# Feature maps of a linear attention: the negative exponentials and the reciprocals moved to GpSimd as powers of -1

## The chip, the cores and the metric

The kernel runs on one core of one Trainium2 chip. The metric is the device time of one execution in microseconds. Three runs of the kernel before gave 747.75, 748.07 and 748.65 us; their median is 748.07 us.

## The reference

Two attention blocks read the same `x` (2048 rows of 512 features, 32 heads of 16) and a gate mixes their outputs. Block A is a linear attention with a feature map of two softmaxes; block B is plain softmax attention. Cut to what matters:

```python
def _A_ref(x, wqkv, w_phi, wo):
    q, k, v = split_heads(x @ wqkv)              # each [B, 32, 2048, 16]
    pq = jnp.einsum("bhsd,hdf->bhsf", q, w_phi)
    pk = jnp.einsum("bhsd,hdf->bhsf", k, w_phi)
    phi_q = jnp.concatenate([_softmax(pq), _softmax(-pq)], axis=-1)   # 32 features of a head
    phi_k = jnp.concatenate([_softmax(pk), _softmax(-pk)], axis=-1)
    kv  = jnp.einsum("bhsf,bhsd->bhfd", phi_k, v)
    z   = jnp.einsum("bhsf->bhf", phi_k)
    num = jnp.einsum("bhqf,bhfd->bhqd", phi_q, kv)
    den = jnp.einsum("bhqf,bhf->bhq", phi_q, z)[..., None] + 1e-6
    return merge_heads(num / den) @ wo

def _B_ref(x, wqkv, wo):
    q, k, v = split_heads(x @ wqkv)
    p = _softmax(jnp.einsum("bhqd,bhkd->bhqk", q, k) * 0.25)
    return merge_heads(jnp.einsum("bhqk,bhkd->bhqd", p, v)) @ wo

g = sigmoid((x * gate_w).sum(-1, keepdims=True))
return g * _A_ref(...) + (1 - g) * _B_ref(...)
```

## The kernel before

**Block B** is most of the work. It is cut into 32 sets (four blocks of 512 queries, four groups of eight heads, two halves of a group), and a set into 16 key tiles of 128 keys. For a key tile TensorE makes four scores of [128 keys, 512 queries] in PSUM (L1106), something turns them into exponentials, and TensorE multiplies them with the values into `psO` (L1143). A key tile is done in one of two ways:

- ScalarE: two exponentials of 128x1024 elements from PSUM into `E` tiles (L1116); then four matmuls with the values.
- VectorE: four operations of 128x512 elements from PSUM write the exponent's bits straight into an int16 tile `T` (L1121), two more of 128x2048 elements from SBUF to SBUF add shifts to it (L1129, tiles `TS`, called "sh" in the code), and three groups of four matmuls add up the three versions.

Up to six key tiles of a set (`DSET`) may go either way; a planner decides.

**Block A** runs beside it. The function `phi` makes a feature map of 128 rows: TensorE projects them (`fill`, L787, tile of 128x512 in PSUM), ScalarE makes exp(P) and exp(-P) in two operations (L979) into the two halves of a bf16 tile of 128x1024, GpSimd sums groups of 16 by halving in four additions (L985, L990, L991, L992), VectorE takes the reciprocals of the 64 sums (L994), and GpSimd multiplies the tile by them (L995). `phi` is called 16 times for the keys (tiles `phk`; their results go to the matmuls of L1018, in four batches) and then 16 times for the queries (tiles in the place of `WAT`; their results are transposed by a DMA and go to the matmuls of L1055).

**The order.** The whole program is recorded as operations with a cost and a priority, and `_Sched` orders it before it is built. `STYLES` holds one seed for each 4 us of the plan; a seed draws the tolerances by which TensorE's next operation is picked in that window (0 is the standard style). Each engine then runs its own queue in that fixed order, with semaphores between engines. The planner knows of a path that GpSimd shares with the shift operations of VectorE: it does not place an operation of GpSimd into the time of a shift, places one that it takes to be longer than `LONG` (0.8 us) close behind a shift (`NEAR`, `HOLD`), and makes the operation of GpSimd wait for the last shift planned ahead of it. A shift is not made to wait for GpSimd:

```python
            elif o.eng == "pool":
                if self.sh and self.sh[-1] not in o.deps and self.sh[-1].end > w - 20.0:
                    o.deps.append(self.sh[-1])
                self.port["pool"] = w + occ + PORT
            elif o.kind == "sh":
                self.sh.append(o)
                self.port["dve"] = w + occ + PORT
```

A general path for large inputs stands behind a flag at the end of the program; with the inputs here it isn't taken.

Of the kernel before, what the change touches and what calls it, by code (L numbers as in the profile page):

```python
# [7 lines left out]
F32 = mybir.dt.float32  # L8
I16 = mybir.dt.int16
I32 = mybir.dt.int32  # L10
ACTF = mybir.ActivationFunctionType
ALU = mybir.AluOpType
# [31 lines left out]
NE_, NPH = 12, 6  # L44
WINDOW = 4.0
STYLES = (
# [11 lines left out]
LEAD = {"act": 1.1, "dve": 1.0}  # L58
NE = "dve"
PORT, LONG, NEAR, HOLD = 0.05, 0.8, 0.3, 6.0  # L60
# [41 lines left out]
class _Sched:  # L102
# [5 lines left out]
    def add(self, eng, prio, occ, fn, deps=(), tiles=(), mode=None, name="", lat=None, dma=None, lane=None, nb=0.0,  # L108
            kind=None, run=None, alt=None):
        o = _Op()  # L110
        o.alt = alt
        o.eng, o.fn, o.occ, o.prio = eng, fn, occ, prio
        o.lat = {"pe": 0.17, "act": 0.12, "dve": 0.09, "pool": 0.1, "sp": 0.0}[eng] if lat is None else lat
        if dma is not None:
            o.lat = dma
        o.deps = [d for d in deps if d is not None]
        o.tiles = list(tiles)
        o.mode, o.name, o.dma, o.lane, o.est, o.kind, o.run = mode, name, dma, lane, nb, kind, run
        o.users, o.start, o.end, o.count, o.sem, o.vc = [], None, None, None, None, None
        o.seq = len(self.ops)  # L120
        for t in o.tiles:
            t.ops.append(o)
        self.ops.append(o)
        return o
# [502 lines left out]
def _build(ctx, nc, A_x, A_wqkv, A_w_phi, A_wo, B_wqkv, B_wo, gate_w, out):  # L627
    cnt = [0]

    def sb(shape, dt=BF16, name="sb"):  # L630
        cnt[0] += 1
        return ctx.enter_context(nc.sbuf_tensor(f"{name}_{cnt[0]}", shape, dt))
# [5 lines left out]
    add = sch.add  # L638
# [21 lines left out]
    omg = sb([128, NT], F32, name="omg")  # L660
    ct = sb([128, 112], F32, name="ct")
    flag = sb([128, 1], I32, name="flag")

    qst_r = ring(2, [128, NQ], name="qst")
    qz_r = ring(2, [128, 4, NQ], name="qz")
# [49 lines left out]
    def x_in(c, deps=()):  # L715
# [12 lines left out]
                  deps=[xin[1]], name=f"x{c}", dma=8.5) for c in (2, 3)]  # L728
# [5 lines left out]
    def pool(prio, occ, fn, deps=(), name="", tiles=(), alt=None, nb=0.0):  # L734
        return add("pool", prio, occ, fn, deps=deps, name=name, tiles=tiles, alt=alt, nb=nb)
# [8 lines left out]
    z3 = pool(-99.4, 0.2, lambda e: e.tensor_single_scalar(ta, ta, 16.0, ALU.is_lt), [z2])  # L744
    z4 = pool(-99.3, 0.2, lambda e: e.tensor_tensor(ta, ta, tb, ALU.mult), [z3])
    op_qm = pool(-99.2, 0.2, lambda e: e.tensor_tensor(qmask[:], ta[:, 0:4], ta[:, 4:8], ALU.add), [z4])
    op_ones = pool(-99.05, 0.3, lambda e: e.memset(ones[:], 1.0))
    op_qz0 = [pool(-60, 1.8, lambda e: e.memset(qz_r.aps[1 - q_t[0, 0].idx], 0.0))]
    vfl = vB[:].rearrange("p t h c -> p (t h) c")
# [5 lines left out]
                  name="wphi", lane=lambda: ("wphi", 0)) for j in range(8)]  # L755
# [48 lines left out]
    for c in range(2):  # L804
        got = []
        for t in range(KT):
# [3 lines left out]
            f = chain((-100, XT1)[c], calls, 0.11, [xin[c], op_id], [m, xs[c]], "xt")  # L810
# [91 lines left out]
    for w in range(2):  # L902
        for t in range(KT):
            tile = _Tile(M_r)
            prio = st_(WP0 + 0.12 * (4 * w + t))
# [7 lines left out]
            f = add("pe", prio, 0.3, fn, deps=[op_wat] + op_wbd, tiles=[tile], mode="full", name="wp", nb=prio - EARLY)  # L913
# [19 lines left out]
    for c in range(QC):  # L933
        m, f = sumsq(st_(CX0 + 0.3 * c), lambda hh, c=c: xT[:, 2 * hh:2 * hh + 2, NQ * c:NQ * (c + 1)], op_x[c], "x")
        cert.append(add("dve", st_(CX0 + 0.2 + 0.3 * c), 0.62, lambda e, m=m, c=c: e.tensor_reduce(ct[:, c:c + 1], m.ap, AX.X, ALU.max),
                        deps=[f], tiles=[m]))
    for i, (w, dp) in enumerate(((W_Bq, [op_wq[0], op_wq[1]]), (W_Bk, [op_wk[0], op_wk[1]]))):
        m, f = sumsq(st_(CW0 + 0.3 * i), lambda hh, w=w: w[:, 2 * hh:2 * hh + 2, :], dp, "w")
# [3 lines left out]
    for w in range(2):  # L942
        m, f = sumsq(st_(CP0 + 0.3 * w), lambda hh, w=w: Wp[:, w, 2 * hh:2 * hh + 2, :], ev_wp[w], "p")
# [27 lines left out]
    def phi(prio, w, st, ee, ee_deps):  # L971
        tile, ss, tr = _Tile(M_r), _Tile(ss_r), _Tile(tr_r)
        f = fill(prio, tile, 0, lambda t: xT[:, t, 128 * st:128 * (st + 1)], lambda t: Wp[:, w, t, :],
                 ev_wp[0] + ev_wp[1] + op_x[st // 4] + ee_deps, f"pf{w}{st}", [ee])
        if w == 1:
            use_wp1.append(f)
        P = lambda: tile.ap.rearrange("p (h f) -> p h f", f=DH)
        ev = lambda: ee.ap.rearrange("p (h f) -> p h f", f=32)
        ex = [add("act", prio, 0.48, lambda e, s=s: e.activation(ev()[:, :, 16 * s:16 * s + 16], P(), ACTF.Exp, scale=1.0 - 2.0 * s),  # L979
                  deps=[f] + ee_deps, tiles=[tile, ee]) for s in range(2)]  # L980
        eg = lambda: ee.ap.rearrange("p (g f) -> p g f", f=DH)
        v8 = lambda: tr.ap[:, 0:512].rearrange("p (g f) -> p g f", f=8)
        v4 = lambda: tr.ap[:, 0:256].rearrange("p (g f) -> p g f", f=4)
        v2 = lambda: tr.ap[:, 256:384].rearrange("p (g f) -> p g f", f=2)
        p1 = pool(prio + 2, 1.23, lambda e: e.tensor_tensor(v8(), eg()[:, :, 0:8], eg()[:, :, 8:16], ALU.add), ex + use_wat,  # L985
                  tiles=[ee, tr], name="ps1")
        tr2 = _Tile(tr2_r)
        u4 = lambda: tr2.ap[:, 0:256].rearrange("p (g f) -> p g f", f=4)
        u2 = lambda: tr2.ap[:, 256:384].rearrange("p (g f) -> p g f", f=2)
        p2 = pool(prio + 2, 0.92, lambda e: e.tensor_tensor(u4(), v8()[:, :, 0:4], v8()[:, :, 4:8], ALU.add), [p1], tiles=[tr, tr2])  # L990
        p3 = pool(prio + 2, 0.56, lambda e: e.tensor_tensor(u2(), u4()[:, :, 0:2], u4()[:, :, 2:4], ALU.add), [p2], tiles=[tr2])  # L991
        p4 = pool(prio + 2, 0.48, lambda e: e.tensor_tensor(ss.ap[:, 0, :], u2()[:, :, 0], u2()[:, :, 1], ALU.add), [p3],  # L992
                  tiles=[tr2, ss])
        o7 = add("dve", prio + 5, 0.46, lambda e: e.reciprocal(ss.ap[:, 1, :], ss.ap[:, 0, :]), deps=[p4], tiles=[ss])  # L994
        return pool(prio + 6, 1.95, lambda e: e.tensor_tensor(  # L995
            eg(), eg(), ss.ap[:, 1, :].unsqueeze(2).to_broadcast([128, 64, DH]), ALU.mult),
            [o7], tiles=[ee, ss], name="phi")
# [3 lines left out]
    for qd in range(4):  # L1001
        items = []
        for i in range(4):
            st = 4 * qd + i
            prio = st_(PK0 + PK1 * st)
            ph, va = _Tile(phk_r), _Tile(vA_r)
            op = phi(prio, 1, st, ph, [])
            tile = _Tile(M_r)
            f = fill(prio + 2, tile, 0, lambda t, st=st: xT[:, t, 128 * st:128 * (st + 1)], lambda t: W_Av[:, t, :],
                     op_x[st // 4] + [op_wav] + op_vAones, "vAf", [va])  # L1010
            use_wav.append(f)
            ev = add("dve", prio + 2, 0.62, lambda e, va=va, tile=tile: e.tensor_copy(
                va.ap[:, :, 0:64], tile.ap.rearrange("p (g c) -> p g c", c=64)), deps=[f] + op_vAones, tiles=[tile, va], name="vAev")
            items.append((ph, va, op, ev))
        for lo in (0, 4):
# [5 lines left out]
            f = chain(st_(PK0 + 0.5 + PK1 * (4 * qd + 3)), calls, 0.06, [x[2] for x in items] + [x[3] for x in items],  # L1021
                      [tkv] + [x[0] for x in items] + [x[1] for x in items], "kv", 0.0, 4 * PIECE)
# [5 lines left out]
            else:  # L1028
                kvo.append(add("dve", pr, 0.38, lambda e, dst=dst, src=src: e.tensor_tensor(dst, src(), dst, ALU.add),
                               deps=[f] + kvo, tiles=[tkv]))  # L1030
# [9 lines left out]
    for st in range(NT):  # L1040
        x = PQ0 + PQ1 * st if st < 4 else PQ2 + PQ3 * (st - 4)
        prio = st_(x)
        ph, ptt, rA, oA, nd = _Tile(eA_r), _Tile(phT_r), _Tile(rA_r), _Tile(oA_r), [_Tile(M_r), _Tile(M_r)]
        nd[0].mate, nd[1].mate = nd[1], nd[0]
        if st % 4 == 0:
# [4 lines left out]
                 deps=[op_ph] + use_wp1, tiles=[ph, ptt], name="phT", dma=2.6, lane=lambda ptt=ptt, st=st: (("phT", ptt.idx), st))  # L1050

        def nums(e, ptt=ptt, nd=nd):
# [8 lines left out]
            deps=[o3, op_ge], tiles=[rA] + nd, name="den")  # L1061
# [5 lines left out]
            deps=[o5] + use_wav, tiles=[nd[b], rA, oA], name="oA") for b in range(2)]  # L1067
# [11 lines left out]
    for s in range(N_SETS):  # L1079
# [12 lines left out]
        for eng, frac, kt in todo:  # L1092
# [4 lines left out]
            for cc in range(2):  # L1097
# [5 lines left out]
                def qk(e, rs=rs, c=c, kt=kt, g=g, qt=qt):  # L1103
                    ins = None
                    for h in range(2):
# [4 lines left out]
                        name=f"qk{s}.{kt}", kind="qk", run=eng, alt=alt)  # L1110
# [119 lines left out]
    for o in sch.order["pe"]:  # L1230
        if o.kind == "pv":
            s, key = o.run
# [71 lines left out]
```

## Time and profile before

| | |
|---|---|
| median of three runs | 748.07 us |
| the profiled execution | 749.46 us, its span 747.6 us |
| granted TensorE clock, mean | 0.992 |
| ScalarE, busy | 711.6 us (95%) |
| TensorE matmuls, busy | 695.1 us (93%) |
| VectorE, busy | 693.4 us (93%) |
| GpSimd, busy | 193.7 us (26%) |
| ScalarE's exponentials of block B (L1116) | 726 of 128x1024 |
| VectorE's shifts (L1129) | 298 of 128x2048 |
| ScalarE's exponentials of the feature maps (L979) | 64 of 128x512 |
| VectorE's reciprocals of their sums (L994) | 32 of 128x64 |

How the profile's lines are read: PE is TensorE, PEld its weight loads, DVE VectorE, ACT ScalarE, POOL GpSimd. A line of a group reads: source line, engine, operation, tile written<-tile read, partitions x elements, count | busy us, mean ns of one | idle time of the engine just before them, and what ended it. In a timeline the first number is the start in us from the span's start and the second the time in us; "xN" merges N of the same kind in a row. Operations of one engine overlap at their ends, so what one costs its queue is the distance from its start to the next one's start.

### The profile page before, as it was taken

How to read it: one execution, taken by the hardware profiler on the slowest of the kernel's cores; microseconds unless marked ns; L12 is line 12 of the kernel's file. 1: busy time of each engine (PE TensorE's matmuls, PEld its weight loads, DVE VectorE, ACT ScalarE, POOL GpSimd, SP SyncE). 2: the span in 40 equal slices, each digit the busy share in tenths (PEclk: the TensorE clock that was granted, in tenths of full speed). 3: DMA queues.
4: the chain of work that ended last, by engine and by line, in shares of the span. 5: the costliest groups of instructions: out<-in, count | busy, mean ns of one | idle time of the engine just before them, and what ended most of it. 6: DMA issues, size and time to landing. Idle time of an engine off the chain costs nothing.

```text
span 747.6 us, 15606 instructions
## 1 busy us (share of the span) xinstructions
PE 695.1 (93%) x6432; PEld 216.0 (29%) x6432; DVE 693.4 (93%) x1212; ACT 711.6 (95%) x803; POOL 193.7 (26%) x234
## 2 busy tenths in 40 slices
PE   7999999999999989988989999998989999988886
PEld 3333342332322222222222332222222322222222
DVE  3989899999999999999999999999999999999993
ACT  3999799999999999999999999999999999999993
POOL 4165241233344343322322012222212112200000
PEclk8999999999999999999999999999999999999999
DMA  8300000011000000001211221211111211111001
GB/s 210 73 16 9 8 16 15 15 41 33 15 15 15 8 14 10 15 16 30 48 31 30 50 50 36 44 33 33 22 36 40 47 36 37 32 27 8 16 8 32
DMA packets 72157, 23.77 MB, mean 32 GB/s; under 512 B 64016, under 2 KB 72080, under 8 KB 72080
## 3 DMA queue, kind: packets, MB, share of 16 engines
q1 hardware_dynamic: 70736, 22.19, 13.9%
q8 instruction: 52, 0.85, 0.5%
q10 hardware_dynamic: 1344, 0.52, 0.3%
q14 instruction: 25, 0.20, 0.1%
HBM read 4.21 MB, written 2.10 MB: 8 GB/s over the span
## 4 chain that ended last, share of the span: by engine, by line
ACT 65%; PE 26%; DVE 5%; DMA 2%; SPq 1%; issue 0%; DVEq 0%
ACT E L1116 62%; PE psR L1106 10%; PE psO L1143 6%; PE psR L787 4%; PE psR L1205 3%; DVE T L1121 2%; PE psR L849 2%; ACT WAT L979 2%; ACT phk L979 1%; DMA OTT<-OT 1%; DVE TS L1129 1%; SPq L706 1%; DMA T<-in_A_x_dram 1%; PE psR L927 1%; DVE ob L1170 1%
## 5 line engine op out<-in xcount | busy, mean ns | idle before, releaser
L1116 ACT ACTIVATE E<-psR 128x1024 bf16<-128x1024 f32 x726 | 679.8, 1120 | 17.2 <-PE psR L1106 15.8
L1121 DVE TENSOR_SCALAR T<-psR 128x512 int16<-128x512 f32 x596 | 380.8, 683 | 20.8 <-PE psR L1106 16.3
L1106 PE MATMUL psR<-qz,kT 64*128 64x512 bf16 x2048 | 347.5, 386 | 38.3 <-ACT E L1116 28.0
L1129 DVE TENSOR_SCALAR TS<-T 128x2048 int16<-128x2048 int16 x298 | 193.2, 684 | 3.1
L1106 PEld LDWEIGHTS psR<-qz,kT 64*128 64x128 bf16 x2048 | 87.0, 93 | 306.6 <-ACT E L1116 221.3
L1143 PE MATMUL psO<-E,vB 128*18 128x512 bf16 x1452 | 127.1, 382 | 0.0
L1143 PE MATMUL psO<-TS,vS 128*18 128x512 bf16 x1192 | 105.6, 382 | 0.6 <-DVE TS L1129 0.6
L1143 PE MATMUL psO<-T,vB 128*18 128x512 bf16 x596 | 58.7, 384 | 0.0
L985 POOL TENSOR_TENSOR WAT<-WAT 128x512 f32<-128x512 bf16 x16 | 18.5, 1156 | 148.0 <-DVE TS L1129 105.6
L990 POOL TENSOR_TENSOR tr<-WAT 128x256 f32<-128x256 f32 x32 | 23.4, 733 | 94.5 <-DVE TS L1129 94.5
L1143 PEld LDWEIGHTS psO<-E,vB 128*18 128x18 bf16 x1452 | 31.3, 88 | 51.3 <-issue 37.1
L995 POOL TENSOR_TENSOR phk<-phk,ss 128x1024 bf16<-128x1024 bf16 x16 | 30.9, 1930 | 51.5 <-DVE TS L1129 51.5
L995 POOL TENSOR_TENSOR WAT<-WAT,ss 128x1024 bf16<-128x1024 bf16 x16 | 30.9, 1930 | 48.5 <-DVE TS L1129 48.5
L1143 PEld LDWEIGHTS psO<-TS,vS 128*18 128x18 bf16 x1192 | 26.6, 87 | 53.3 <-issue 29.5
L787 PE MATMUL psR<-Wp,xT 128*128 128x512 bf16 x128 | 33.2, 382 | 0.8 <-DVE T L1121 0.8
L787 PE MATMUL psR<-xT,WB 128*128 128x512 bf16 x128 | 33.2, 382 | 0.4 <-ACT WAT L979 0.2
L985 POOL TENSOR_TENSOR WAT<-phk 128x512 f32<-128x512 bf16 x16 | 18.7, 1166 | 31.2 <-DVE TS L1129 31.2
L1143 PEld LDWEIGHTS psO<-T,vB 128*18 128x18 bf16 x596 | 14.5, 87 | 27.9 <-issue 21.4
L862 POOL TENSOR_SCALAR vS<-vB 128x144 bf16<-128x144 bf16 (+1 forms) x32 | 11.9, 373 | 39.4 <-DVE TS L1129 34.0
L770 DVE CAST OT<-psO 128x512 bf16<-128x512 f32 x31 | 21.1, 681 | 0.1
L979 ACT ACTIVATE phk<-psR 128x512 bf16<-128x512 f32 x32 | 18.6, 675 | 0.8 <-PE psR L787 0.8
L979 ACT ACTIVATE WAT<-psR 128x512 bf16<-128x512 f32 x32 | 19.1, 709 | 0.0
(108 smaller groups left out, 379.7 us busy)
## 6 DMA issues: line engine op xcount, KB each, us to landing
qz<-qst SPq DMA_DIRECT2D x120, 16.0 KB, 1.8
out_dram<-WAv SPq DMA_DIRECT2D x12, 128.0 KB, 1.7
WB<-in_B_wqkv_dram SPq DMA_DIRECT2D x3, 384.0 KB, 6.7
T<-in_A_x_dram SPq DMA_DIRECT2D x2, 512.0 KB, 5.3
WAv<-in_A_wqkv_dram SPq DMA_DIRECT2D x1, 512.0 KB, 8.3
WB<-in_A_wo_dram SPq DMA_DIRECT2D x1, 512.0 KB, 3.9
WB<-in_B_wo_dram SPq DMA_DIRECT2D x1, 512.0 KB, 3.6
OTT<-OT SPq DMA_TRANSPOSE x31, 2.4
```

The source lines that it names most:

```text
L770: return add("dve", prio, 0.6, lambda e: e.tensor_copy(dst(), src()), deps=deps, tiles=tiles, name=name)
L787: calls = [lambda e, t=t: e.matmul(tile.ap[:, off:off + 512], lhsT=lhs(t), rhs=rhs(t), start=(t == 0), stop=(t == KT - 1)) for t in range(KT)]
L979: ex = [add("act", prio, 0.48, lambda e, s=s: e.activation(ev()[:, :, 16 * s:16 * s + 16], P(), ACTF.Exp, scale=1.0 - 2.0 * s), deps=[f] + ...
L985: p1 = pool(prio + 2, 1.23, lambda e: e.tensor_tensor(v8(), eg()[:, :, 0:8], eg()[:, :, 8:16], ALU.add), ex + use_wat, tiles=[ee, tr], nam ...
L990: p2 = pool(prio + 2, 0.92, lambda e: e.tensor_tensor(u4(), v8()[:, :, 0:4], v8()[:, :, 4:8], ALU.add), [p1], tiles=[tr, tr2])
L995: return pool(prio + 6, 1.95, lambda e: e.tensor_tensor(eg(), eg(), ss.ap[:, 1, :].unsqueeze(2).to_broadcast([128, 64, DH]), ALU.mult), [o ...
L1106: ins = e.matmul(rs[h].ap, lhsT=kT[64 * h:64 * h + 64, g, 128 * kt:128 * (kt + 1)], rhs=qt.ap[64 * h:64 * h + 64, c, :], start=True, stop= ...
L1116: exps.append(add("act", pr + 0.5 * cc, 0.905, lambda e, rs=rs, E=E: e.activation(E.ap.rearrange("p (a n) -> p a n", n=512), pair(rs), ACT ...
L1121: exps.append(add("dve", pr + 0.5 * cc + 0.01 * h, 0.6, lambda e, rs=rs, T=T, cc=cc, h=h: e.tensor_scalar(T.ap[:, 1024 * cc + 512 * h:1024 ...
L1129: s1, s2 = (add("dve", pr + 1.0 + 0.3 * m, 0.6, lambda e, T=T, X=X, m=m: e.tensor_single_scalar(X.ap, T.ap, SHIFT[m], ALU.add), deps=exps, ...
L1143: ins = e.matmul(O.ap[32 * col:32 * col + VW, :], lhsT=lhs(hd), rhs=rhs(cc)[:, 512 * h:512 * (h + 1)], start=(first_pv[s] == key), stop=(l ...
L1205: calls = [lambda e, tile=tile, off=off, sl=sl, src=src, w=w, n=n: e.matmul(tile.ap[:, off:off + 512], lhsT=src.ap[:, n % 4, sl], rhs=w[:, ...
```

## The change

`phi` makes exp(-P) on GpSimd, as exp(P) to the power -1 (a TENSOR_TENSOR of 512 elements a partition against a tile of -1), in place of the second exponential on ScalarE. It also makes the reciprocals of the 64 sums on GpSimd, as the sums to the power -1, in place of VectorE's reciprocal. A tile `neg1` of -1 is set once at the start. With new seeds in `STYLES` the planner orders the whole program anew; in the new plan 728 of block B's exponentials on ScalarE and 296 shifts on VectorE remain to be done, one key tile going from VectorE to ScalarE. Line numbers behind `neg1` move on by one or two: the power for exp(-P) is L981, that of the sums L996, the first addition L987, the last multiplication L997, VectorE's shifts L1131.

```diff
-STYLES = (0, 0, 0, 382076, 683899, 331868, 616951, ...
+STYLES = (0, 0, 0, 409401, 114659, 18674, 912595, ...
...
+    neg1 = sb([128, 64], F32, name="neg1")
...
+    op_neg1 = pool(-99.06, 0.2, lambda e: e.memset(neg1[:], -1.0))
...
     P = lambda: tile.ap.rearrange("p (h f) -> p h f", f=DH)
     ev = lambda: ee.ap.rearrange("p (h f) -> p h f", f=32)
-    ex = [add("act", prio, 0.48, lambda e, s=s: e.activation(ev()[:, :, 16 * s:16 * s + 16], P(), ACTF.Exp, scale=1.0 - 2.0 * s),
-              deps=[f] + ee_deps, tiles=[tile, ee]) for s in range(2)]
+    e1 = add("act", prio, 0.48, lambda e: e.activation(ev()[:, :, 0:16], P(), ACTF.Exp), deps=[f] + ee_deps, tiles=[tile, ee])
+    ex = [e1, pool(prio + 1, 1.2, lambda e: e.tensor_tensor(ev()[:, :, 16:32], ev()[:, :, 0:16], neg1[:, 0:16].unsqueeze(1).to_broadcast([128, 32, 16]),
+                                                           ALU.pow), [e1, op_neg1], tiles=[ee], name="inv")]
...
-    o7 = add("dve", prio + 5, 0.46, lambda e: e.reciprocal(ss.ap[:, 1, :], ss.ap[:, 0, :]), deps=[p4], tiles=[ss])
+    o7 = pool(prio + 5, 0.4, lambda e: e.tensor_tensor(ss.ap[:, 1, :], ss.ap[:, 0, :], neg1[:], ALU.pow), [p4, op_neg1], tiles=[ss])
```

21 rows, old and new, of the table STYLES are left out of this document.

## The prediction

> **What bounds the kernel now.** I read the page's busy times first, then stretches of 100 us, the chain that ended last, the waits, the groups with shapes kept apart, and the timelines of VectorE and GpSimd around the feature maps. Engines by stretch (columns: stretch, us, then busy us and count of each engine, TensorE's clock, DMA share, GB/s):
>
> ```profile
> 300.00:400.00 100.00, 90.64 (x858) 26.40 (x852) 95.62 (x173) 99.60 (x114) 25.89 (x29) 1.00 0.15 30
> 400.00:500.00 100.00, 96.88 (x863) 28.53 (x860) 95.12 (x169) 99.11 (x113) 22.53 (x25) 1.00 0.18 38
> 500.00:600.00 100.00, 93.09 (x842) 26.72 (x840) 96.95 (x175) 99.63 (x113) 19.92 (x22) 1.00 0.19 37
> ```
>
> ScalarE (fourth of the busy times) is full at 99 to 100 of 100 us, VectorE (third) at 95 to 97, TensorE at 91 to 97. ScalarE sets the pace, but VectorE has only 3 to 5% to spare: what holds VectorE up comes out in the end time almost whole. The chain that ended last says the same: "ACT 65%; PE 26%; DVE 5%". GpSimd is a quarter busy, but not a quarter used: it waits.
>
> ```profile
> POOL WAT L985 <- DVE TS L1129: 136.9, 19, 13.4
> POOL tr L990 <- DVE TS L1129: 94.5, 32, 5.9
> POOL phk L995 <- DVE TS L1129: 51.5, 16, 5.5
> POOL WAT L995 <- DVE TS L1129: 48.5, 16, 5.4
> ```
>
> (Waits: who waited for whom, us in total, times, longest.) GpSimd's long operations each wait for a shift of VectorE to end, since the planner puts them into the gaps between pairs of shifts. The reason is in the trace, where one plan went wrong; VectorE and GpSimd around 190 us:
>
> ```profile
> 189.34 0.69 DVE L1129 TENSOR_SCALAR TS<-T 128x2048 int16<-128x2048 int16 x1
> ...
> 190.28 1.10 DVE L1129 TENSOR_SCALAR TS<-T 128x2048 int16<-128x2048 int16 x1
> ```
> ```profile
> 190.11 0.73 POOL L990 TENSOR_TENSOR tr<-WAT 128x256 f32<-128x256 f32 x1 [1.79 <-DVE TS L1129]
> ```
>
> The second shift started 0.17 us into an addition of GpSimd and took 1.10 us where its twin took 0.69: it stood until about when the addition ended (190.84) and then ran. So a shift waits out an operation of GpSimd that is under way. One sentence of the Trainium skill, SBUF — State Buffer, Who interferes with whom, says the same as a rule: of a VectorE operation in a two-port mode and a GpSimd operation, whoever issues first has the shared pair of ports for its whole instruction, and the other fully blocks. By that rule, which this pair bears out, a long operation of GpSimd costs VectorE whatever is left of it when the next shift comes.
>
> How long may it be? VectorE in the keys' stage:
>
> ```profile
> 247.16 0.54 DVE L994 RECIPROCAL ss<-ss 128x64 f32<-128x64 f32 x1
> 247.62 1.23 DVE L1129 TENSOR_SCALAR TS<-T 128x2048 int16<-128x2048 int16 x2
> 248.93 1.29 DVE L1121 TENSOR_SCALAR T<-psR 128x512 int16<-128x512 f32 x2
> ...
> 252.05 1.29 DVE L1129 TENSOR_SCALAR TS<-T 128x2048 int16<-128x2048 int16 x2
> ```
>
> GpSimd is let go at 248.93 (L995 starts there) and the next pair of shifts comes at 252.05: a gap of 3.1 us, and 3.0 in the next one (253.42 to 256.42). Call it 3.0.
>
> **What it takes off.** ScalarE loses 32 exponentials. Their 0.69 us are not their cost, since operations overlap:
>
> ```profile
> 323.30 1.13 ACT L979 ACTIVATE WAT<-psR 128x512 bf16<-128x512 f32 x2
> 324.26 18.51 ACT L1116 ACTIVATE E<-psR 128x1024 bf16<-128x1024 f32 x20
> 342.49 1.26 ACT L979 ACTIVATE WAT<-psR 128x512 bf16<-128x512 f32 x2
> ```
>
> From start to start the pair takes 0.96 us, so one takes 0.48, and an exponential of block B (342.49 - 324.26) / 20 = 0.91. So ScalarE loses 32 x 0.48 = 15.4 us and gains 2 x 0.91 = 1.8: net -13.6. VectorE loses 32 reciprocals of 0.46 us (247.16 to 247.62), 14.7, and one key tile, four operations of 0.60 and two of 0.65, 3.7: -18.4. TensorE loses eight matmuls with the values at 127.1 / 1452 = 0.09 us: -0.7. Its 52.5 idle us can take in a run that is 13 us shorter, but not for nothing: TensorE would be 94.5% busy instead of 93%. Of ScalarE's 13.6 I count 11 on the path. The new order by itself I count at nothing: the feature maps keep their places (109 of block B's exponentials ahead of the first, 110 before; 107 behind the last, as before); bounds of plus and minus 4 us for it, the 5.4 us of the longest single wait of ScalarE being the scale. The setting of `neg1` lies in the first 25 us, when GpSimd is 31% busy and nothing waits for it.
>
> **What it adds.** 32 powers of 512 elements and 32 of 64 on GpSimd. No row of this trace shows a power. The rows near it:
>
> ```profile
> L990 POOL TENSOR_TENSOR tr<-WAT 128x256 f32<-128x256 f32 x32 | 23.4, 733 | 94.5 <-DVE TS L1129 94.5
> L985 POOL TENSOR_TENSOR WAT<-phk 128x512 f32<-128x512 bf16 x16 | 18.7, 1166 | 31.2 <-DVE TS L1129 31.2
> L862 POOL TENSOR_SCALAR vS<-vB 128x288 bf16<-128x288 bf16 x16 | 6.9, 433 | 34.5 <-DVE TS L1129 34.0
> L739 POOL TENSOR_SCALAR ident<-ident 128x128 f32<-128x128 f32 x1 | 0.6, 550 | 0.0
> ```
>
> The floor is an addition of as many elements, 1.16 us. But on GpSimd the operation counts, not only the size: two multiplications (L862) run at (433 - 314) / 144 = 0.83 ns an element, the comparison of L739 at (550 - 381) / 64 = 2.6. And the row nearest in kind, the reciprocal that the power replaces, takes 541 ns for 64 elements and 345 for 32 (L1062), 6.1 ns an element, where a plain conversion takes (683 - 420) / 256 = 1.03: six times. GpSimd's addition has 0.2 us of start (L745, 8 elements) and 0.95 / 512 = 1.9 ns an element; six times that is 11 ns, so a power of 512 takes 0.2 + 5.7 = 5.9 us and one of 64 takes 0.9. With the 2.6 ns of the float rows (733 against 400 for half as many) it is 15.6 ns and 8.2 us. So bounds of 1.16 and 8.2 us; I take 5.9, since a power with a free exponent is no simpler than a reciprocal. The Trainium skill, GPSIMD Engine Reference, Elementwise — side-by-side cycle accounting, says that a loop body there is bound by its ports up to two operations an element and from three on runs roughly three operations a cycle, at 1.2 GHz. An estimate by that page: each three further steps are 0.43 us for 512 elements, and some 13 more steps than the addition's bring 1.16 us to the gap's 3.0; no row shows how many a power takes.
>
> Where that time goes: GpSimd alone could bear it (194 + 32 x 6.8 = 411 us of 748), but a power begins behind a pair of shifts, and the next pair stands until it ends: 5.9 - 3.0 = 2.9 us, 32 times, 93 us on VectorE. Behind the shifts stand VectorE's exponentials and evacuations, for the shifted tiles waits TensorE in order, and for TensorE's scores ScalarE; VectorE's 3 to 5% idle, some 20 us over the stages from 128 to 636 us, takes some of it in. Against that, only 14 of the 32 powers carry a wait for VectorE of their own in the new queue of GpSimd; 18 follow something else in the same gap, mostly an addition or a multiplication of 1.2 to 1.9 us: 18 x 1.2 = 22 more. I set these two off. The reciprocals' powers (0.9, behind 0.73 + 0.40 + 0.30 us and their hand-overs) just fit a gap and cost nothing; if they miss it, up to 32 x 0.9 = 29. The added hand-over from ScalarE to GpSimd ahead of the sums hides behind the six buffers of `phk`; without them it would be a late batch of L1018 in TensorE's queue, with all of ScalarE's scores behind it.
>
> **The sum.** 749.5 - 11 + 93 = 831.5 in the profiled execution, which stood 1.4 us above the median: 830 us.
>
> **The rivals.**
> - A power costs what an addition costs, 1.2 us: it fits each gap, nothing of VectorE is held up, and it is 749.5 - 11 - 1.4 = 737 us, with its own range from 731 to 742. For it: size and operands are those of L985. Against it: the spread of rates by operation on GpSimd, and the factor six of the reciprocal. The change of sides is at 3.0 + 11 / 32 = 3.3 us for a power of 512. Chance 0.36.
> - The power lies near that point, 2.7 to 3.6 us: 749.5 - 11 - 1.4 to that and 32 x 0.6 more, 737 to 756. Chance 0.06, shared among the three outcomes.
> - The power is a long routine, above 9.5 us: then GpSimd becomes the bound in the keys' stage, where a feature map comes every 11.1 us (128 to 306 us for 16) and takes 4.5 us of other work; at 12 us a power it is 749.5 - 11 + 32 x 9 = 1026 us or more. For it: nothing in the trace bounds the routine from above. Chance 0.16.
> - The change not doing what it says (a power executed as something else, at another price) is inside these prices.
>
> **How the numbers follow.** The case forecast, powers of 3.6 to 9.5 us, has 0.42, and its own range is from 757 to 945. Slower in all is 0.42 + 0.16 + 0.02 = 0.60, faster 0.36 + 0.02 = 0.38, within 0.2% (1.5 us, about what a measurement of this kernel tells from no change) 0.02. The range must reach from the cheap power to a power of 8.2 us, 749.5 - 11 + 32 x 5.2 - 1.4 = 903, and with 29 for reciprocals that miss their gap 932: 731 to 932, leaving out the long routine and little more.
>
> **What would show it.** In the profile after: the group L981 on GpSimd with its mean (5.9 us by the forecast, 1.2 by the rival); L1131's shifts, 296 of them, with a mean near 0.69 + 93 / 296 = 1.0 us and some of 3 us and more; VectorE's busy time raised by that, ScalarE's share down from 95% to about 84%; the reciprocals' group at 0.9 us. If L1131 keeps 0.69 while L981 is long, the rule of the held port is wrong. If L981 is below 3 us, the forecast falls, and ScalarE should be at 95 to 96% of a span near 736 us.

## The result: 3401 us, and the profile after

| | before | after |
|---|---|---|
| median | 748.36 us (747.75 to 750.87, 4 runs) | 3401.09 us (3399.71 to 3401.61, 4 runs) |
| profiled execution, its span | 749.46, 747.6 us | 3400.77, 3398.9 us |
| granted TensorE clock, mean | 0.992 | 0.607 |

The ratio is 4.542 (95% interval 4.532 to 4.552). The page of the kernel after, busy times and three of the rows of 40 slices (tenths):

```profile
PE 733.5 (22%) x6424; PEld 223.4 (7%) x6424; DVE 684.3 (20%) x1174; ACT 705.4 (21%) x773; POOL 3156.4 (93%) x299
...
PE   8900110050002200040021122111223102123208
...
POOL 4599999999999999999999999899998999998980
PEclk9955555585555655575565566565666556567559
```

ScalarE and VectorE do about the work they did before (711.6 and 693.4 us then), spread over 3400 us; GpSimd went from 194 to 3156 us and is full from the first map to the last. The groups that answer to those of before (busy us, mean ns, idle time before them):

```profile
L981 POOL TENSOR_TENSOR WAT<-WAT,neg 128x512 bf16<-128x512 bf16 x16 | 1312.5, 82031 | 37.9 <-DVE TS L1131 37.9
L981 POOL TENSOR_TENSOR phk<-phk,neg 128x512 bf16<-128x512 bf16 x16 | 1313.1, 82067 | 12.6 <-DVE TS L1131 12.6
...
L996 POOL TENSOR_TENSOR ss<-ss,neg 128x64 f32<-128x64 f32 x32 | 338.2, 10569 | 2.4
...
L1131 DVE TENSOR_SCALAR TS<-T 128x2048 int16<-128x2048 int16 x296 | 197.7, 705 | 4.4 <-PE psO L1145 1.1
```

A power of 512 elements takes 82.0 us and one of 64 takes 10.6: 71 and 35 times the additions of the same sizes (1.16 and 0.30 us). The shifts kept 0.705 us. GpSimd's timeline shows one map:

```profile
134.48 82.07 POOL L981 TENSOR_TENSOR phk<-phk,neg 128x512 bf16<-128x512 bf16 x1 [12.60 <-DVE TS L1131]
216.69 1.15 POOL L987 TENSOR_TENSOR WAT<-phk 128x512 f32<-128x512 bf16 x1
...
219.64 10.56 POOL L996 TENSOR_TENSOR ss<-ss,neg 128x64 f32<-128x64 f32 x1
...
231.06 1.93 POOL L997 TENSOR_TENSOR phk<-phk,ss 128x1024 bf16<-128x1024 bf16 x1
232.95 82.24 POOL L981 TENSOR_TENSOR phk<-phk,neg 128x512 bf16<-128x512 bf16 x1
```

From one power to the next it is 98.5 us, where the maps of the keys came every 11.1 us in the kernel before. The first power starts at 134.5 us and the last multiplication ends at 3304.9: 3170 us for 32 maps, 99 each. With the 134.5 us ahead of them and 94 behind (99 in the kernel before) that is the whole span. The other engines wait for the maps in their fixed order (waits: us in total, times, longest; "issue" stands where the profile shows nothing that the engine waited for):

```profile
ACT E L1118 <- PE psR L1108: 2595.3, 89, 347.0
...
PE psR L1020 <- POOL phk L997: 1128.6, 4, 345.5
...
PE psR L1057 <- issue: 789.6, 10, 82.2
PE psR L1057 <- DMA Wp<-WAT: 391.9, 5, 81.6
```

TensorE stands at each batch of the keys' matmuls (L1020) and at the maps of the queries (L1057), which reach it through the transposing DMA; ScalarE stands behind TensorE. ScalarE's 2595 us are put down to TensorE, and not to GpSimd: the wait must be followed over two steps.

### The profile page after: what moved, and what is told of

Read it like the earlier page. It is cut to its first block, busy times and chain, and to the rows that moved or that the text cites. A ratio compares the mean times of both kernels' runs of the same rounds, so it can differ in the third digit from the quotient of the medians.

```text
span 3398.9 us, 15636 instructions
## 1 busy us (share of the span) xinstructions
PE 733.5 (22%) x6424; PEld 223.4 (7%) x6424; DVE 684.3 (20%) x1174; ACT 705.4 (21%) x773; POOL 3156.4 (93%) x299
## 4 chain that ended last, share of the span: by engine, by line
POOL 57%; issue 31%; PE 5%; ACT 4%; DVE 2%; DMA 0%; SPq 0%; POOLq 0%; ACTq 0%
POOL phk L981 24%; POOL WAT L981 22%; POOL ss L996 8%; ACT E L1118 4%; PE psR L1108 2%; PE psO L1145 1%; DVE T L1123 1%; POOL phk L997 1%; POOL WAT L987 1%; DVE TS L1131 1%; PE psR L788 1%; POOL tr L992 1%; POOL WAT L997 1%; PE psR L1207 0%; POOL tr L993 0%
## 5 line engine op out<-in xcount | busy, mean ns | idle before, releaser
L981 POOL TENSOR_TENSOR WAT<-WAT,neg 128x512 bf16<-128x512 bf16 x16 | 1312.5, 82031 | 37.9 <-DVE TS L1131 37.9
L981 POOL TENSOR_TENSOR phk<-phk,neg 128x512 bf16<-128x512 bf16 x16 | 1313.1, 82067 | 12.6 <-DVE TS L1131 12.6
L1118 ACT ACTIVATE E<-psR 128x1024 bf16<-128x1024 f32 x728 | 687.6, 1074 | 2597.6 <-PE psR L1108 2595.3
L1108 PE MATMUL psR<-qz,kT 64*128 64x512 bf16 x2048 | 358.9, 405 | 26.5 <-ACT E L1118 16.3
L996 POOL TENSOR_TENSOR ss<-ss,neg 128x64 f32<-128x64 f32 x32 | 338.2, 10569 | 2.4
L1057 PE MATMUL psR<-kz,Wp 128*128 128x68 bf16 x128 | 9.6, 240 | 1181.6 <-issue 789.6
L1020 PE MATMUL psR<-vA,phk 128*128 128x65 bf16 x128 | 7.9, 244 | 1128.6 <-POOL phk L997 1128.6
L1131 DVE TENSOR_SCALAR TS<-T 128x2048 int16<-128x2048 int16 x296 | 197.7, 705 | 4.4 <-PE psO L1145 1.1
L1057 PEld LDWEIGHTS psR<-kz,Wp 128*128 128x128 bf16 x128 | 7.4, 125 | 1186.6 <-issue 1186.2
L1020 PEld LDWEIGHTS psR<-vA,phk 128*128 128x128 bf16 x128 | 7.2, 131 | 1130.5 <-issue 1129.7
L863 POOL TENSOR_SCALAR vS<-vB 128x144 bf16<-128x144 bf16 (+1 forms) x32 | 11.8, 371 | 38.3 <-DVE TS L1131 33.0
L1171 DVE RECIPROCAL rB<-OTT 128x16 f32<-128x16 bf16 x31 | 7.6, 245 | 158.4 <-DMA OTT<-OT 158.4
```

Of the source, the lines that this page charges most:

```text
L981: ex = [e1, pool(prio + 1, 1.2, lambda e: e.tensor_tensor(ev()[:, :, 16:32], ev()[:, :, 0:16], neg1[:, 0:16].unsqueeze(1).to_broadcast([12 ...
L996: o7 = pool(prio + 5, 0.4, lambda e: e.tensor_tensor(ss.ap[:, 1, :], ss.ap[:, 0, :], neg1[:], ALU.pow), [p4, op_neg1], tiles=[ss])
L1057: ins = e.matmul(nd[g // 4].ap[:, 68 * (g % 4):68 * (g % 4) + 68], lhsT=ptt.ap[:, g, :], rhs=kz[:, g, :], start=True, stop=True)
L1108: ins = e.matmul(rs[h].ap, lhsT=kT[64 * h:64 * h + 64, g, 128 * kt:128 * (kt + 1)], rhs=qt.ap[64 * h:64 * h + 64, c, :], start=True, stop= ...
L1118: exps.append(add("act", pr + 0.5 * cc, 0.905, lambda e, rs=rs, E=E: e.activation(E.ap.rearrange("p (a n) -> p a n", n=512), pair(rs), ACT ...
L1131: s1, s2 = (add("dve", pr + 1.0 + 0.3 * m, 0.6, lambda e, T=T, X=X, m=m: e.tensor_single_scalar(X.ap, T.ap, SHIFT[m], ALU.add), deps=exps, ...
```

## The experiments

Two theories stood after the trace: the price of the power alone made the time, through GpSimd's queue; or, as the prediction had it, a long operation of GpSimd holds VectorE's shifts. And one term of the prediction was untested: what the change is worth apart from the price of the power.

**The same order with cheap operations.** Each power becomes a multiplication:

```diff
-    ALU.pow), [e1, op_neg1], tiles=[ee], name="inv")]
+    ALU.mult), [e1, op_neg1], tiles=[ee], name="inv")]
...
-    o7 = pool(prio + 5, 0.4, lambda e: e.tensor_tensor(ss.ap[:, 1, :], ss.ap[:, 0, :], neg1[:], ALU.pow), [p4, op_neg1], tiles=[ss])
+    o7 = pool(prio + 5, 0.4, lambda e: e.tensor_tensor(ss.ap[:, 1, :], ss.ap[:, 0, :], neg1[:], ALU.mult), [p4, op_neg1], tiles=[ss])
```

> The kernel after, instruction for instruction and in the same order, but both powers are multiplications by the same tile of -1 (so the negative exponentials and the reciprocals hold wrong numbers). Theory (the price of the power alone made the time; plan and moves are sound): L981 at about 1.2 us, L996 at 0.3, and the cheap rival's time of the prediction, 737 us (731 to 742). Rival (the moves or the new order cost time whatever the power costs, because the negative half now passes through GpSimd's queue): 748 us or more.

Measured 743.57 us (6 runs, 742.20 to 744.76) against 749.07, ratio 0.992 (0.990 to 0.994). So all of the loss is the price of the power: 3401.1 - 743.6 = 2657.5 us, and from the first of L981 to the end of the last of L997 GpSimd takes 512 us here (135.9 to 647.6) and 3170 in the kernel after, 2658 more. But the gain was half of what the prediction's sum had: 5.5 us, not 11. The chain that ended last is ScalarE's again (57%), and its waits in this run read

```profile
ACT E L1118 <- PE psR L1108: 22.4, 40, 5.5
```

and in the kernel before

```profile
ACT E L1116 <- PE psR L1106: 15.8, 28, 5.4
```

In the profiled executions ScalarE's busy time fell by 11.8 us (711.6 to 699.8), its waits for scores rose by 6.6, and the span fell by the difference, 5.2. Whether the moved work or the new order made the waits longer is not shown.

**Tangents in place of powers.** A second kernel in the same order:

```diff
+    ex = [e1, pool(prio + 1, 1.2, lambda e: e.tensor_scalar(ev()[:, :, 16:32], ev()[:, :, 0:16], -1.0, 2.0, op0=ALU.mult, op1=ALU.add), ...
...
+    o7 = pool(prio + 5, 0.4, lambda e: e.tensor_scalar(ss.ap[:, 1, :], ss.ap[:, 0, :], -1.0 / 256.0, 0.125, op0=ALU.mult, op1=ALU.add), ...
```

> The kernel after in the same order, with a one-input operation in place of each power: 2 - e for 1/e (e is an exponential near 1 with these inputs) and 1/8 - s/256 for 1/s (s is a sum near 16), each the tangent, good only for feature maps near zero. Theory: L981 at about 0.65 us (512 elements at 0.83 ns and 0.2 to start), time within 3 us of the multiplications' run, so 734 to 740 us. Rival (the moves cost): 748 us or more.

Measured 743.07 us (6 runs), ratio 0.992 (0.990 to 0.993), above the 734 to 740 that I expected but within 1 us of the multiplications; L981 at 0.62 to 0.64 us, where a multiplication took 1.17. It is 0.8% below the kernel before, but good only for feature maps as near zero as these; the flag for the general path was not narrowed to that, so it is no version to keep as it stands. That it is level with the multiplications' run says that 0.5 us of GpSimd more or less, 32 times, changes nothing here.

**The price by itself.** A program without attention: GpSimd's operations one behind the other, then the same kinds beside shifts of VectorE that follow each other without a pause.

> GpSimd alone, no attention in it: additions of 512 float elements, powers of 64, 128 and 256 elements, of bf16 and float, with base 1, with exponents 1 and 2, on 16 partitions and on one; then additions, multiplications and powers beside VectorE that runs shifts of 128x2048 without a pause. Theory (a general routine, some 160 ns an element whatever the numbers): 10.5, 20.8 and 41.2 us for 64, 128 and 256 elements, 41 us for each other form of 256, on 16 partitions too. Rival (the exponent -1 or the type is a slow special case): exponents 1 or 2 or bf16 stand apart by a factor of two or more. On the port: by the prediction's rule no shift ends while a power runs, so shifts of 10 and 80 us; by the trace of the kernel after, shifts inside a power keep 0.69 us and only one at its start or end is held, by about 1.2 us. Beside additions and multiplications shifts are held in both views.

Powers of 64, 128 and 256 elements took 10.56, 20.77 and 41.23 us: 159.7 ns an element and 0.3 us to start. For 256 elements bf16 took 41.18, base 1 41.23, exponents 1 and 2 41.23 each, 16 partitions and one partition 41.22 each. So in no form tried did the exponent, the base, the type or the number of partitions matter, as the theory of a general routine has it. GpSimd's timeline for two of the pairs:

```profile
163.88 82.53 POOL L58 TENSOR_TENSOR pow256exp<-x,plus 128x256 f32<-128x256 f32 x2
246.48 82.51 POOL L58 TENSOR_TENSOR pow256part<-x,minus 16x256 f32<-16x256 f32 x2
```

The second half did not answer its question: GpSimd's first addition came to an end only when VectorE had done all its shifts.

```profile
329.03 138.56 DVE L73 TENSOR_SCALAR TS<-T 128x2048 int16<-128x2048 int16 x230 [329.03 <-POOL pow256part L58]
```
```profile
335.28 148.16 POOL L63 TENSOR_TENSOR with_add<-x,minus 128x512 f32<-128x512 f32 x12 [6.29 <-DVE TS L73]
```

The first of the twelve took 133.4 us and ended 1.1 us after the last shift (467.6); the others took 1.26 each. So no power ran beside a shift here. The unbroken row of shifts shut the addition out, which neither view had.

**Do ordinary operations hold shifts?** The kernel before without the planner's waits:

```diff
                 if self.sh and self.sh[-1] not in o.deps and self.sh[-1].end > w - 20.0:
-                    o.deps.append(self.sh[-1])
+                    pass
```

> The kernel before, without the waits by which GpSimd's operations stand behind a shift of VectorE (they order no data). If ordinary operations of GpSimd hold shifts, as the one pair at 190 us showed: some tens of the 298 shifts are held, by 0.3 to 1.9 us, mean of L1129 from 0.69 to about 0.75 to 0.85 us, time 750 to 765 us. If they do not: L1129 keeps 0.69, time 748 us or a little less.

Measured 801.73 us, ratio 1.071 (1.069 to 1.072), more than I expected. The shifts in the kernel before, and then in this run:

```profile
L1129 DVE TENSOR_SCALAR TS<-T 128x2048 int16<-128x2048 int16 x298 | 193.2, 684 | 3.1
```
```profile
L1129 DVE TENSOR_SCALAR TS<-T 128x2048 int16<-128x2048 int16 x298 | 252.1, 881 | 3.1
```

The mean shift went from 684 to 881 ns: 298 x 0.197 = 59 us of shifts, and the time rose by 53. 47 shifts took more than 0.8 us, up to 2.42, and each of them ended 0.55 us behind the end of the operation of GpSimd that was under way when it began (L862, L922, L985, L990 or L995). So ordinary operations do hold shifts, to their end. VectorE's busy time rose by 53.0 us in the profiled execution (693.4 to 746.4) and the span by 50.7: what held VectorE up passed into the time almost whole, as the prediction said. The power is another matter. In the kernel after, VectorE and GpSimd around a power of 64 and the start of one of 512:

```profile
717.24 1.89 DVE L1131 TENSOR_SCALAR TS<-T 128x2048 int16<-128x2048 int16 x3
719.04 2.48 DVE L1123 TENSOR_SCALAR T<-psR 128x512 int16<-128x512 f32 x4
721.55 2.26 DVE L1131 TENSOR_SCALAR TS<-T 128x2048 int16<-128x2048 int16 x2
```
```profile
711.25 11.08 POOL L996 TENSOR_TENSOR ss<-ss,neg 128x64 f32<-128x64 f32 x1
721.77 82.37 POOL L981 TENSOR_TENSOR phk<-phk,neg 128x512 bf16<-128x512 bf16 x1
```

Three shifts at 717.24 ran through the power of 64 in 1.89 us, as without it. Of the pair at 721.55 the second began 0.39 us into the power of 512, took 1.65 us, and so got its path about 1.35 us into it, with 81 us of it still to come. Counted over the trace, some 195 shifts lie wholly inside a power (from 2 us after its start), at a mean of 687 ns.

**The powers one at a time.** First the reciprocals alone, with the seeds of before:

```diff
-        o7 = add("dve", prio + 5, 0.46, lambda e: e.reciprocal(ss.ap[:, 1, :], ss.ap[:, 0, :]), deps=[p4], tiles=[ss])
+        o7 = pool(prio + 5, 0.4, lambda e: e.tensor_tensor(ss.ap[:, 1, :], ss.ap[:, 0, :], neg1[:], ALU.pow), [p4, op_neg1], tiles=[ss])
```

> The kernel before with the reciprocals alone as powers on GpSimd (64 elements, 10.6 us each by the trace of the kernel after); exp(-P) stays on ScalarE; the planner orders it with the seeds of before. Theory (GpSimd's queue is what ends late; a power holds up no shift): the keys' maps take 16 x (4.5 + 10.6 + 0.6) = 251 us of GpSimd in place of 181, the queries' maps come every 19.6 us and fit: about +70 us, 800 to 830. Rival (the prediction's held port): each power holds the next shifts for 10.6 - 3.0 us, 32 times, +243: 990 us, with L1129 at a mean of 1.5 us.

Measured 949.58 us (one run): between the two, and nearer the rival's number, but not by its mechanism. The shifts are at 746 ns, not 1500: 302 x 0.06 = 18 us. Not one of the 16 shifts of more than 0.8 us was held by a power: each ended 0.55 us behind an addition or a multiplication (L987, L992, L997). 30 shifts began in the first 2 us of a power of 64, the earliest 0.22 us into it, and all of them took less than 0.7 us. The rest is mostly TensorE standing in its queue, 147 us in these two waits (PEld is its weight load):

```profile
PEld psR L1057 <- issue: 76.0, 15, 7.0
PEld psR L1020 <- issue: 70.5, 6, 19.8
```

From the first exponential of the maps to the last multiplication the keys took 276 us in place of 193, and the queries 438 in place of 326, although GpSimd had time for the latter (245 us of work in those 438). TensorE stood at the queries' matmuls for up to 7 us, 15 times. If that is because the planner's price is wrong, so that each map comes later than the order has it, the true price should end it; the next kernel tells the planner 10.6 us:

```diff
-        o7 = pool(prio + 5, 0.4,
+        o7 = pool(prio + 5, 10.6,
```

> The kernel with the reciprocals alone as powers, but with the planner told 10.6 us for each in place of 0.4. That kernel took 949.58 us with the wrong price: 275 us for the 16 maps of the keys (181 in the kernel before) and 420 for those of the queries (some 325), with TensorE's queue standing at the matmuls of each map of the queries by up to 7 us. Theory (the queries' loss is only the order: a map ready 10 us later than planned stands TensorE's queue, though GpSimd has the time): the queries' stage comes back to about 330 us, the keys' stage stays at some 255 us, since GpSimd's work is 16 x 16 us; 820 to 850 us. Rival (shifts held by GpSimd, or GpSimd's load, cost it): 930 us or more.

Measured 845.05 us (one run), in the theory's range, and the waits it named are gone:

```profile
PEld psR L1057 <- issue: 0.7, 3, 0.2
PEld psR L1020 <- issue: 0.9, 3, 0.4
```

The split by stages that I expected is not there to compare: this order lets the queries' maps begin (278 us) before those of the keys are done (485 us), and moves 19 key tiles from VectorE to ScalarE against the run just before (760 exponentials, 264 shifts). The remaining 97 us over the kernel before are settled in part only: ScalarE is busy for 34 us more (746.0 for 711.6, with 34 more exponentials of block B) and idle for 61 more, mostly in waits for TensorE. Why TensorE is late is open.

Then the negative exponentials alone:

```diff
-        o7 = pool(prio + 5, 0.4, lambda e: e.tensor_tensor(ss.ap[:, 1, :], ss.ap[:, 0, :], neg1[:], ALU.pow), [p4, op_neg1], tiles=[ss])
+        o7 = add("dve", prio + 5, 0.46, lambda e: e.reciprocal(ss.ap[:, 1, :], ss.ap[:, 0, :]), deps=[p4], tiles=[ss])
```

> The kernel after with the negative exponentials alone as powers; the reciprocals go back to VectorE. Theory (queue): 134 us ahead of the first power, 32 x (82.0 + 4.5 + 1.7 for hand-overs and VectorE's reciprocal) = 2822, some 96 behind the last: 3050 us. If the two powers hid behind each other it would stay near 3400.

Measured 3206.45 us (one run), 156 above the theory's sum. The two powers add up as work: GpSimd is busy 2818 us, 338 less than in the kernel after, which is 32 x 10.6. But the hand-over was sized too small. GpSimd is idle for 387 of 3205 us, against 243 in the kernel after: the reciprocal now stands in VectorE's queue until the sums come, with the shifts behind it that GpSimd's next operation waits for. The reciprocal's waits, and the largest of GpSimd's for a shift:

```profile
DVE ss L996 <- POOL ss L994: 2176.2, 25, 152.7
```
```profile
POOL WAT L981 <- DVE TS L1131: 109.6, 13, 15.5
```

**Was it the order?** The planner is told both measured prices:

```diff
-        ex = [e1, pool(prio + 1, 1.2, ...
+        ex = [e1, pool(prio + 1, 82.1, ...
-        o7 = pool(prio + 5, 0.4, ...
+        o7 = pool(prio + 5, 10.6, ...
```

> The kernel after with the planner told the measured prices, 82.1 and 10.6 us, in place of 1.2 and 0.4. Theory (GpSimd's own work is the bound, 32 x 97.9 = 3133 us): the order can move only what lies ahead of the first power and behind the last, 3250 to 3400 us. Rival (what costs is the order that was made with wrong prices, since TensorE's queue runs into waits): well under that, 2000 us or less.

Measured 3447.67 us (one run), a little above the range and 47 above the kernel after. Where GpSimd's own work exceeds the time, knowing its price saves nothing.

**What the seeds are worth.** The multiplications' kernel with the seeds of before, and the kernel before with the seeds of after; only `STYLES` is exchanged.

> The kernel with both powers made multiplications (743.57 us in the new order), planned with the seeds of the kernel before. The two orders have the same work but for the key tiles that the planner moves. If the new seeds hold the gain: 748 us or more here. If the gain is in the work taken off ScalarE and VectorE and the seeds hardly matter: 739 to 746 us.

> The kernel before, its feature maps as they were, planned with the seeds of the kernel after. The prediction counted the new order at nothing, with bounds of 4 us either way: 744 to 752 us. If seeds must be drawn for the very work they order: more than 752 us.

Measured 764.58 us, ratio 1.020 (1.017 to 1.023), and 772.28 us, ratio 1.032 (1.030 to 1.034). Either list of work loses by the other's seeds: 764.6 - 743.6 = 21 us and 772.3 - 748.4 = 24 us. With the seeds of before, the moved work is 16 us slower than the kernel before (764.6 for 748.4), and not faster.

## Why the prediction was wrong

- **What bounds the kernel** held: in the run without waits VectorE was busy for 53.0 us more and the span grew by 50.7, and ScalarE was the bound again in the run with multiplications.
- **What it takes off** (step "of ScalarE's 13.6 I count 11 on the path") was mis-sized: 5.5 us came of it. ScalarE's work did fall by 11.8, but its waits for TensorE's scores rose by 6.6. The cheap rival's range, 731 to 742, missed its own case (743.6).
- **The new order "at nothing", plus or minus 4 us**, did not hold as it was put: an exchange of the seeds alone costs 24 us on the work of before and 21 on that of after, five times the bound. These are the prices of seeds on work that they were not drawn for. What an order drawn for the new work is worth against one drawn for the old cannot be told apart from the work taken off: the 5.5 us are both together, and either change without the other is a loss.
- **What it adds** is the step that failed first. The floor was an addition's 1.16 us and the upper bound six times an addition's rate, 8.2 us, by VectorE's reciprocal. Measured: 82.0 us, ten times the bound, and 10.6 for 0.9. With these in the text's own count of GpSimd's load, 194 + 32 x 6.8 us, it comes to 194 + 32 x 92.6 = 3157, and 3156 was measured: GpSimd could not bear it within 748 us. The text itself said, under the long routine, that nothing in the trace bounds the price from above, and then let the range end at a price from another engine's hardware. That rival had 0.16, and its mechanism, GpSimd as the bound, is what happened. At 82 us its sum gives 749.5 - 11 + 32 x 79 = 3267, near the 3401 by luck: it counts a power less the gap of 3 us and leaves the reciprocals' 10.6 out. What the span is made of is 134.5 us, 32 maps of 99 on GpSimd, and 94.
- **Where that time goes** failed too: a power was to hold the next shifts until it ends. One of 512 elements holds them for its first 1.0 to 1.4 us only, and one of 64 held none that began 0.2 us or more into it. The forecast shift of 1.0 us came out at 0.705. The single pair of shifts at 190 us was rightly read, and the run without waits bears it out for additions and multiplications; it did not carry over to the power, and no run shows why. The rule of the Trainium skill, SBUF — State Buffer, Who interferes with whom, that the pair of ports is held for the whole instruction, agrees with the run without waits (shifts of 0.88 us) and differs from the power's (some 195 shifts inside it at 0.687); for the power the measurement decides.
- **Slower** was forecast with 0.60, and slower it is, but the sign is right by another path than the forecast's case: the cost did not come by VectorE, as the prediction had it, but by GpSimd's queue and TensorE's fixed order behind it.

## What to carry to other kernels

An operation with no row in any trace has no upper bound from rows of other operations, least of all from those of another engine: run it once by itself before a plan is made round it, or let the range say that it is open. On an idle engine in an ordered pipeline count latency as well as load: with a wrong price in the plan, reciprocals of 10.6 us cost 200 us; with the right one, 97 (one run each). And seeds that were drawn for one list of work belong to it: a change and its new order must be tried, and counted, together.

## What the runs showed of the hardware that was not expected

- GpSimd's power takes 159.7 ns an element of a partition and 0.3 us to start; at 256 elements it was the same within 0.1 us for fp32 and bf16, bases 1 and 1.5, exponents -1, 1 and 2, and 128, 16 and 1 partitions. By the three operations a cycle at 1.2 GHz of the Trainium skill, GPSIMD Engine Reference, Elementwise — side-by-side cycle accounting, that would be some 575 operations an element, as an estimate; no run shows what they are.
- A power of 512 leaves VectorE's shifts alone after 1.0 to 1.4 us (the starts of held shifts in the traces of the kernel after and of the one with negative exponentials alone), a power of 64 after 0.2 us or less (the run with the reciprocals alone); additions and multiplications hold them to the end (all 47 long shifts of the run without waits).
- An unbroken row of 220 shifts on VectorE let an addition of GpSimd through only behind the last of them: 133.4 us in place of 1.26, in the one case tried.
- With the engines waiting for GpSimd the granted TensorE clock stood at 0.56 to 0.60 in the means of four stretches from 110 to 3000 us (0.99 to 1.00 in the kernel before from 110 us on), and the scores' matmuls took 405 ns in place of 386 over the whole run.
